# A weight split on one Trainium2 core: the rescaling as a leaky rectifier that also places the sign bit, and one VectorE step less

## The chip, the cores and the metric

The kernel runs on one core of a Trainium2 chip. The metric is the device time of one launch in microseconds (us). The kernel before was run three times: 892.18, 892.35 and 892.69 us, median 892.35 us.

## What is computed

The reference runs three layers one after the other. The first is attention in a sliding window of 64 positions (4 batches, 8 heads, 576 positions, head dimension 64). The second is `softplus(x @ w_in) @ w_out` with 512, 2048 and 512 features for 2304 tokens. The third is a gated layer with three weight matrices:

```python
h = x @ w_in
g = np.maximum(h, 0.0) + np.log1p(np.exp(-np.abs(h)))
x = g @ w_out
gate = 1.0 / (1.0 + np.exp(-(x @ w_gate)))
val = x @ w_val
out = gate * val @ w_out2
```

The weights arrive as 64-bit floats, which the kernel reads as pairs of 32-bit words.

## The kernel before, in words

**Products.** Every product is made with three matrix multiplies, since each factor is split into a high part and a low part (`mm3`, L405 to L408: high by high, high by low, low by high). The first layer runs in five token blocks of 512, 384, 384, 512 and 512 (`BLOCKS1`). For each block and each of 16 slices `f` of the hidden features, `m1_proj(b, f)` makes 12 multiplies into one of two PSUM banks (`h0`, `h1`, chosen by `f % 2`). Then `m1_act` (L435) is the Softplus on ScalarE, `g_hi` (L442) rounds to the high part on ScalarE, `g_lo` (L448) takes the low part on VectorE, and `m1_out(b, f)` makes 12 multiplies into the four accumulators. TensorE runs `m1_proj(f)`, `m1_out(f - 2)`, `m1_proj(f + 1)` and so on in a fixed list (`slots`). Therefore `m1_proj(f + 2)` needs the bank that `g_lo(f)` frees.

**Attention.** The eight groups of block 0 are worked at the start. Those of a later block `b` are worked in the time of block `b - 1`: scores (TensorE, L290), maximum (VectorE, L304 and L307), exponentials (ScalarE, L317, four per group), sum and reciprocal (VectorE, L325 and L326), scaling (GpSimd, L331). Then the probabilities are transposed. For block 1 that is four multiplies on TensorE per group (L339) and a copy (L368); for later blocks VectorE and DMAs do it. The products with the values follow on TensorE (L388), then `att_hi` (L397) and `att_lo` (L402).

**Weights.** Weights come in pairs of 128x512 (two single ones at the start, and single ones for the last matrix). `w_load` (L136) loads them on SyncE's queue. Then five steps make the two parts. `w_scale` (L161, ScalarE) takes the upper word as a 32-bit float and multiplies by 2 to the minus 112, which moves the exponent. `w_shift` (L165, VectorE) shifts the result left by three bits. `w_sign` (L169, VectorE) puts the sign bit of the upper word in. `w_low` (L174, VectorE) puts the three upper bits of the lower word in. `w_hi` (L180, ScalarE) rounds to the high part, and `w_lo` (L188) takes the low part, once per weight. The weights of the first layer are made while block 0 runs. In the time of blocks 1 to 4 the gate and value weights go through the same steps up to `w_low` and then into sums that are sent to DRAM (`c_sums`, `c_hi`, `c_lo`, `c_send`). The twelve single weights of the last matrix follow after that.

**Order.** Each engine runs its instructions in the order in which they are written. Up to the end of the first layer that order comes from a planner, `lead_in` (L957). It asks `traits` (L799) for each step's engine, its estimated time, what it needs and which buffers it takes, derives due times backward from TensorE's list, and then places the step that can start soonest, or the most urgent of those that can start almost as soon. For ScalarE it tells two kinds apart, `"act exp"` and `"act soft"`, and adds 1.3 us (`SWITCH`) where the kind changes; `w_scale` is plain `"act"`:

```python
if engine == "act" and need and need[0] != table:
    us += SWITCH
```

The ACT_TABLE_LOAD instructions themselves are placed when the program is built; the kernel writes one only, at L1030.

Of the kernel before, what the change touches and what calls it, by code (L numbers as in the profile page):

```python
# [9 lines left out]
F32 = mybir.dt.float32  # L10
# [3 lines left out]
AF = mybir.ActivationFunctionType  # L14
ALU = mybir.AluOpType
# [27 lines left out]
def tile_kernel(ctx: ExitStack, tc: tile.TileContext, qk, vt, w1, w2, wg, wv, wo, out):  # L43
# [20 lines left out]
    nc = tc.nc  # L64
# [50 lines left out]
    pair_t, raw_t, bits_t, w_t = {}, {}, {}, {}  # L115

    def pair(slot, turn, dtype, *shape):
        key = slot // 2, turn
        if key not in pair_t:
            pair_t[key] = wpool.tile([P, 2, *shape], dtype, tag=f"w{slot // 2}", name=f"w{slot // 2}", bufs=1)  # L120
        return pair_t[key]

    def size(i):
        return 2 if 1 < i < WO_AT else 1
# [13 lines left out]
    def raw(i, k):  # L138
        r = raw_t[i - i % 2].rearrange("p c (n two) -> p c n two", two=2)
        return r[:, i % 2:i % 2 + size(i), :, k]  # L140

    def bits(i):
        if i == 1:
            bits_t[i] = bits_t["first"][:, 1:]
        if i not in bits_t:
            u, n = i // 2, size(i)
            if u < 3:
                t = main.tile([P, 2, DM], U32, tag="g", name="bits", bufs=GB)
                bits_t.setdefault("first", t)
            elif 4 <= u < 14:  # L150
                slot = 14 + u % 4 // 2 if u < 12 else 15
                t = pair(2 * slot, -20 - u // 2, U32, 2 * DM)[:, u % 2].rearrange("p (c n) -> p c n", c=2)
            else:
                t = main.tile([P, 2, DM], U32, tag="bits", name="bits", bufs=1)
            bits_t[i] = t[:, :n]
        return bits_t[i]
# [1 line left out]


    def w_scale(i):  # L160
        nc.scalar.activation(out=bits(i).bitcast(F32), in_=raw(i, 1).bitcast(F32), func=AF.Copy, scale=2.0 ** -112)  # L161

    def w_shift(i):
        t = bits_t[i]
        nc.vector.tensor_scalar(out=t, in0=t, scalar1=3, scalar2=None, op0=ALU.logical_shift_left)  # L165

    def w_sign(i):
        t = bits_t[i]
        nc.vector.scalar_tensor_tensor(out=t, in0=raw(i, 1), scalar=0x80000000, in1=t, op0=ALU.bitwise_and,  # L169
                                       op1=ALU.bitwise_or)  # L170

    def w_low(i):
        t = bits_t[i]
# [457 lines left out]
    def at(slot, order, fn, *args):  # L631
        events[slot].append((order, len(events[slot]), fn, args))
# [50 lines left out]
    for b in range(1, NB1):  # L683
        s0, s1 = pos[m1_proj, b - 1, 0], pos[m1_proj, b, 0]
        ng, g0 = BLOCKS1[b] // Q, starts1[b] // Q
        for j in range(ng):
            far = b >= FAR
            first = -3 if far else 9
            t = s0 + first + (s1 - s0 - (14 if far else 15 + first)) * (j // 2) // max(ng // 2 - 1, 1)
# [4 lines left out]
    def weight(i, t):  # L694
        for k in range(size(i)):
            at(t - 2, 50, w_load, i + k)
        at(t, -20, w_scale, i)
        at(t + 1, -20, w_shift, i)
        at(t + 1, -19, w_sign, i)
        at(t + 1, -18, w_low, i)  # L700
        at(t + 2, -20, w_hi, i)
        for k in range(size(i)):
            at(t + 2, -19, w_lo, i + k)

    for i in (0, 1, *range(2, len(seq1), 2)):
        weight(i, i + LAG - (i < 3) * (3 - i) - LEAD)
# [3 lines left out]
    def used_last(slot):  # L710
        return max(pos[m1_proj if kind == "w1" else m1_out, NB1 - 1, f]
                   for (kind, f), _ in seq1[slot - slot % 2:slot - slot % 2 + 2])

    for f in range(NF2):
        t, i = COMBO0 + int(COMBO * f), len(seq1) + 2 * f
        at(t - 2, -60, w_load, i)
        at(t - 1, -60, w_load, i + 1)
        at(t, -20, w_scale, i)
        at(t + 1, -20, w_shift, i)
        at(t + 1, -19, w_sign, i)  # L720
        at(t + 1, -18, w_low, i)
        at(t + 3, -15, c_sums, f)
        at(t + 4, -15, c_sum4, f)
        for k, part in enumerate(("a", "v", "x", "s4")):
            at(t + 2 + k, -14, c_hi, f, part)
            at(t + 2 + k, -13, c_lo, f, part)
            at(t + 6 + k, -61, c_send, f, part)
    for f in range(NF2):
        i = WO_AT + f
        t = end + (-7, -1)[f] if f < 2 else pos[m2_out, 0, f - 2, 0] - 1  # L730
        t0 = t - 8
        assert used_last(place[i]) < t < pos[m2_out, 0, f, 0] - 4, (f, used_last(place[i]), t, pos[m2_out, 0, f, 0])
        at(t0, -60, w_load, i)
        at(t, -20, w_scale, i)
        at(t + 1, -20, w_shift, i)
        at(t + 2, -20, w_sign, i)
        at(t + 3, -20, w_low, i)
        at(t + 4, -20, w_hi, i)
        at(t + 4, -19, w_lo, i)
    at(last + 4, -62, wc_load, 0, 0)  # L740
    at(end, -62, wc_load, 0, 1)
    for s in range(NS2):
        t = last + 2 if s == 0 else pos[m2_prod, s - 1, 3, 0]
# [5 lines left out]
    for k in range(7):  # L749
        for kc in range(2):  # L750
            t = max(used_last(2 * k + kc) + 1, last + 18 + k)
# [27 lines left out]
    for g in range(NG0):  # L779
        t = int(first + RG * g)  # L780
# [18 lines left out]
    def traits(fn, a, *rest):  # L799
# [71 lines left out]
            return "act", 0.12 + 0.48 * size(a), deps, ring  # L871
        if fn is w_shift:
            return "dve lock", 0.15 + 0.27 * size(a), [(w_scale, a)], []
        if fn in (w_sign, w_low):
            return "dve lock", 0.15 + 0.54 * size(a), [(w_shift if fn is w_sign else w_sign, a)], []
        if fn is w_hi:
            deps, u = [(w_low, a)], a // 2
            if a >= WO_AT:
# [78 lines left out]
    def lead_in():  # L957
# [5 lines left out]
        for t in sorted(events):  # L963
            if t < end:
                us = when[t] if t >= 0 else OPEN + 2.9 * t
                for order, n, fn, args in sorted(events.pop(t), key=lambda e: e[:2]):
                    nodes[fn, *args] = [us + order / 400, *traits(fn, *args)]
# [122 lines left out]
```

## Time and profile before

| | |
|---|---|
| median of three runs | 892.35 us |
| profiled execution, own time | 892.14 us |
| its span | 890.3 us |
| granted TensorE clock, mean | 0.999 of full speed |
| TensorE busy | 882.0 us, 99% of the span |
| VectorE busy | 522.9 us, 59% |
| ScalarE busy | 398.2 us, 45% |
| GpSimd busy | 154.7 us, 17% |
| DMA | 177.57 MB, mean 199 GB/s |

The profile shows one execution. "Busy" counts time in instructions that compute; a multiply's end is modelled, so 99% for TensorE says that it hardly ever stood still. The span is the time from the first to the last profiled instruction; what the metric has beyond it (1.84 us here) lies around the program. PE is TensorE, DVE is VectorE, ACT is ScalarE, POOL is GpSimd and SP is SyncE.

### The profile page before, as it was taken

The numbers are of one execution on the slowest core, as the hardware profiler recorded it, in microseconds if no ns is written. First come the engines' busy times: TensorE is split into PE (matmuls) and PEld (weight loads), VectorE is DVE, ScalarE is ACT, GpSimd is POOL, SyncE is SP. The second block draws the span as 40 slices with busy tenths as digits, with TensorE's granted clock in tenths as the row PEclk, the third lists the DMA queues.
The fourth block names the chain that finished last, engine by engine and source line by source line (L and its number), as shares of the span: only waits on it lengthen the run. The fifth ranks groups of instructions, "written<-read, shape, count | busy, mean of one in ns | idle before, by whom it ended". The sixth has DMA issues, their size and how long they took to land.

```text
span 890.3 us, 13467 instructions
## 1 busy us (share of the span) xinstructions
PE 882.0 (99%) x5035; PEld 795.9 (89%) x5035; DVE 522.9 (59%) x907; ACT 398.2 (45%) x878; POOL 154.7 (17%) x157
## 2 busy tenths in 40 slices
PE   9999999999999999999999999999999999999997
PEld 7788889999999888888889999999999999999996
DVE  5899976556646657365515667667445447444444
ACT  6867866537755656245323333334222225122222
POOL 4001201102110121003001233331111112111110
PEclk9999999999999999999999999999999999999999
DMA  9946446657886764773306665545454445444441
GB/s 349 396 160 219 136 161 219 244 171 248 270 267 229 234 229 157 229 261 131 131 18 242 243 252 206 201 179 212 185 204 156 156 157 221 173 166 166 166 166 72
DMA packets 56209, 177.57 MB, mean 199 GB/s; under 512 B 6096, under 2 KB 21456, under 8 KB 51536
## 3 DMA queue, kind: packets, MB, share of 16 engines
q1 hardware_dynamic: 56000, 176.58, 56.0%
q8 instruction: 40, 0.66, 0.3%
q14 instruction: 25, 0.20, 0.1%
q10 hardware_dynamic: 144, 0.13, 0.0%
HBM read 139.72 MB, written 36.96 MB: 198 GB/s over the span
## 4 chain that ended last, share of the span: by engine, by line
PE 93%; DMA 4%; DVE 2%; ACT 1%; issue 0%; SPq 0%; ACTq 0%
PE h L406 17%; PE h L408 17%; PE h L407 17%; PE acc L406 11%; PE acc L407 11%; PE acc L408 11%; PE at L290 2%; PE at L408 2%; PE at L407 2%; PE at L406 2%; PE at L388 2%; DMA raw<-in_w 1%; DMA w<-in_w 1%; DMA w<-in_vt 1%; DMA w<-in_qk 1%; DVE w L174 0%
## 5 line engine op out<-in xcount | busy, mean ns | idle before, releaser
L524 DVE TENSOR_TENSOR w<-h,w 128x384 f32<-128x384 f32 x216 | 117.1, 556 | 160.1 <-PE h L408 157.4
L406 PE MATMUL h<-w,wc 128*128 128x384 f32 x504 | 169.0, 335 | 0.1
L408 PE MATMUL h<-w,wc 128*128 128x384 f32 x504 | 169.0, 335 | 0.0
L407 PE MATMUL h<-w,wc 128*128 128x384 f32 x504 | 168.8, 335 | 0.0
L536 POOL TENSOR_TENSOR g<-w,g 128x384 fp32r<-128x384 f32 x70 | 74.0, 1057 | 296.8 <-ACT g L529 252.1
L406 PE MATMUL h<-xt,w 128*128 128x512 f32 (+1 forms) x320 | 119.1, 372 | 0.4 <-ACT w L180 0.3
L406 PE MATMUL acc<-g,w 128*128 128x512 f32 (+1 forms) x320 | 119.4, 373 | 0.0
L408 PE MATMUL h<-xt,w 128*128 128x512 f32 (+1 forms) x320 | 117.9, 368 | 0.5 <-DVE w L188 0.5
L408 PE MATMUL acc<-g,w 128*128 128x512 f32 (+1 forms) x320 | 117.6, 368 | 0.0
L407 PE MATMUL acc<-g,w 128*128 128x512 f32 (+1 forms) x320 | 117.6, 368 | 0.0
L407 PE MATMUL h<-xt,w 128*128 128x512 f32 (+1 forms) x320 | 117.6, 368 | 0.0
L448 DVE TENSOR_TENSOR g<-h,g 128x512 fp32r<-128x512 f32 (+1 forms) x80 | 50.7, 633 | 83.3 <-ACT g L442 82.9
L406 PEld LDWEIGHTS h<-w,wc 128*128 128x128 f32 x504 | 94.6, 188 | 2.3 <-DVE w L524 0.4
L407 PEld LDWEIGHTS h<-w,wc 128*128 128x128 f32 x504 | 94.6, 188 | 2.0
L408 PEld LDWEIGHTS h<-w,wc 128*128 128x128 f32 x504 | 94.6, 188 | 0.0
L529 ACT CAST g<-w 128x384 fp32r<-128x384 f32 x72 | 36.9, 513 | 119.1 <-DVE w L524 119.1
L435 ACT ACTIVATE h<-h 128x512 f32<-128x512 f32 (+1 forms) x80 | 43.2, 540 | 104.6 <-PE h L408 104.3
L408 PEld LDWEIGHTS h<-xt,w 128*128 128x128 f32 x320 | 60.1, 188 | 8.9 <-DVE w L188 1.4
L406 PEld LDWEIGHTS h<-xt,w 128*128 128x128 f32 x320 | 60.1, 188 | 8.6 <-issue 0.6
L331 POOL TENSOR_TENSOR p<-p,st 128x512 f32<-128x512 f32 (+1 forms) x28 | 29.2, 1049 | 220.8 <-DVE st L326 107.6
L406 PEld LDWEIGHTS acc<-g,w 128*128 128x128 f32 x320 | 60.1, 188 | 7.7
L408 PEld LDWEIGHTS acc<-g,w 128*128 128x128 f32 x320 | 60.1, 188 | 7.5
(129 smaller groups left out, 1433.6 us busy)
## 6 DMA issues: line engine op xcount, KB each, us to landing
wc<-wcd SPq DMA_DIRECT2D x36, 1792.0 KB, 7.4
qk<-in_qk SPq DMA_DIRECT2D x28, 512.0 KB, 4.9
wcd<-raw SPq DMA_DIRECT2D x24, 512.0 KB, 3.2
w<-in_w SPq DMA_DIRECT2D x16, 512.0 KB, 9.2
raw<-in_w SPq DMA_DIRECT2D x16, 512.0 KB, 4.6
v<-in_vt SPq DMA_DIRECT2D x25, 256.0 KB, 3.6
raw<-in_wg SPq DMA_DIRECT2D x12, 512.0 KB, 5.1
raw<-in_wv SPq DMA_DIRECT2D x12, 512.0 KB, 6.7
```

What stands on the lines that cost most here:

```text
L290: nc.tensor.matmul(out=s[:, j, :w], lhsT=t[:, 0, j, :], rhs=t[:, 1, j, :w], start=g >= NG0, stop=g >= NG0 or j == NPAIR - 1)
L331: nc.gpsimd.tensor_tensor(out=p[:, :, :w], in0=p[:, :, :w], in1=st[:, 2, :].unsqueeze(2).to_broadcast([P, NPAIR, w]), op=ALU.mult)
L388: nc.tensor.matmul(out=o[h * Q:(h + 1) * Q, j, k * Q:(k + 1) * Q], lhsT=v[:w, (2 * j + h) * Q:(2 * j + h + 1) * Q], rhs=pt[:w, h, j], star ...
L406: nc.tensor.matmul(out=o, lhsT=lh, rhs=rh, start=first, stop=False)
L407: nc.tensor.matmul(out=o, lhsT=lh, rhs=rl, start=False, stop=False)
L408: nc.tensor.matmul(out=o, lhsT=ll, rhs=rh, start=False, stop=last)
L435: nc.scalar.activation(out=t, in_=t, func=AF.Softplus)
L448: nc.vector.tensor_tensor(out=g[:, 1, :n], in0=t, in1=g[:, 0, :n].bitcast(F32), op=ALU.subtract)
L524: nc.vector.tensor_tensor(out=out, in0=a, in1=b, op=op)
L529: nc.scalar.copy(out=g[:, 0, :HALF], in_=t)
L536: eng.tensor_tensor(out=g[:, 1, :HALF], in0=t, in1=g[:, 0, :HALF].bitcast(F32), op=ALU.subtract)
```

## The change

`w_scale` no longer uses Copy but Prelu, a rectifier with a slope of its own for negative inputs. A positive word is multiplied by 2 to the minus 112 as before. A negative one is multiplied further by minus 2 to the 32: the result is positive, and its exponent is larger by 32. The shift by three bits carries that bit of the exponent into the place of the sign. `w_sign` is removed, with its three calls and its place in `traits`; `w_low` now follows `w_shift` directly, also in the planner. Nothing else in the planner's table is edited: `w_scale` stays plain `"act"` with the same estimated time.

```diff
     def w_scale(i):
-        nc.scalar.activation(out=bits(i).bitcast(F32), in_=raw(i, 1).bitcast(F32), func=AF.Copy, scale=2.0 ** -112)
+        nc.scalar.activation(out=bits(i).bitcast(F32), in_=raw(i, 1).bitcast(F32), func=AF.Prelu, scale=2.0 ** -112,
+                             alpha=-2.0 ** 32)
...
-    def w_sign(i):
-        t = bits_t[i]
-        nc.vector.scalar_tensor_tensor(out=t, in0=raw(i, 1), scalar=0x80000000, in1=t, op0=ALU.bitwise_and,
-                                       op1=ALU.bitwise_or)
...
         at(t + 1, -20, w_shift, i)
-        at(t + 1, -19, w_sign, i)
         at(t + 1, -18, w_low, i)
...
         at(t + 1, -20, w_shift, i)
-        at(t + 2, -20, w_sign, i)
         at(t + 3, -20, w_low, i)
...
-        if fn in (w_sign, w_low):
-            return "dve lock", 0.15 + 0.54 * size(a), [(w_shift if fn is w_sign else w_sign, a)], []
+        if fn is w_low:
+            return "dve lock", 0.15 + 0.54 * size(a), [(w_shift, a)], []
```

## Rows read from the trace of the kernel before

**Rows 1.** The page: busy time of the engines (share of the span), instructions.
```profile
PE 882.0 (99%) x5035; PEld 795.9 (89%) x5035; DVE 522.9 (59%) x907; ACT 398.2 (45%) x878; POOL 154.7 (17%) x157
```

**Rows 2.** Timeline of TensorE: start, length, line, tile; idle before and releaser in brackets.
```profile
27.18 2.76 PE L418 MATMUL h<-idle 128*128 128x512 bf16 x12
30.10 0.47 PE L406 MATMUL h<-xt,w 128*128 128x512 f32 x1
...
37.79 0.50 PE L406 MATMUL h<-xt,w 128*128 128x512 f32 x1 [0.26 <-ACT w L180]
...
93.38 0.50 PE L408 MATMUL h<-xt,w 128*128 128x512 f32 x1 [0.53 <-DVE w L188]
```

**Rows 3.** Stages: stretch, its length, busy of PE, PEld, DVE, ACT, POOL (counts).
```profile
34.00:66.00 32.00, 31.74 (x147) 26.14 (x147) 29.85 (x41) 23.60 (x43) 0.00 (x0) 1.00 0.63 226
66.00:106.00 40.00, 39.47 (x251) 32.75 (x250) 36.50 (x57) 32.91 (x66) 7.16 (x6) 1.00 0.54 181
130.00:370.00 240.00, 240.00 (x1579) 223.52 (x1578) 137.53 (x253) 141.29 (x338) 35.49 (x34) 1.00 0.68 226
475.00:890.00 415.00, 410.45 (x2149) 382.55 (x2148) 227.08 (x408) 119.11 (x238) 88.84 (x82) 1.00 0.50 185
```

**Rows 4.** Stages, VectorE's sign step (L169) alone: stretch, its length, busy (count).
```profile
0.00:106.00 106.00, 16.37 (x14) 1.00 0.71 255
106.00:890.00 784.00, 27.31 (x27) 1.00 0.55 192
```

**Rows 5.** SyncE's queue: what the weight loads waited for (us, times, longest).
```profile
SPq L136 <- DVE w L174: 41.4, 8, 12.6
```

**Rows 6.** ScalarE's groups by line: the table loads (busy, mean ns, idle before).
```profile
L435 ACT ACT_TABLE_LOAD x15 | 19.2, 1283 | 0.3
L317 ACT ACT_TABLE_LOAD x14 | 18.0, 1283 | 0.8 <-DVE st L307 0.5
```

**Rows 7.** Timeline of ScalarE, 65 to 85 us, columns as in Rows 2.
```profile
65.38 0.58 ACT L435 ACTIVATE h<-h 128x512 f32<-128x512 f32 x1
65.99 0.59 ACT L442 CAST g<-h 128x512 fp32r<-128x512 f32 x1
66.48 1.14 ACT L161 ACTIVATE w<-raw 128x1024 f32<-128x1024 f32 x1
...
68.45 0.59 ACT L435 ACTIVATE h<-h 128x512 f32<-128x512 f32 x1
...
69.56 1.15 ACT L161 ACTIVATE w<-raw 128x1024 f32<-128x1024 f32 x1
73.78 0.58 ACT L435 ACTIVATE h<-h 128x512 f32<-128x512 f32 x1 [3.08 <-PE h L408]
...
75.82 1.18 ACT L161 ACTIVATE w<-w 128x1024 f32<-128x1024 f32 x1
...
80.11 0.58 ACT L435 ACTIVATE h<-h 128x512 f32<-128x512 f32 x1 [1.05 <-PE h L408]
...
82.79 1.28 ACT L317 ACT_TABLE_LOAD   x1 [0.53 <-DVE st L307]
84.09 0.40 ACT L317 ACTIVATE p<-p,st 128x128 f32<-128x128 f32 x1
```

**Rows 8.** Timelines of GpSimd and TensorE: the scaled probabilities and their transposes.
```profile
88.03 3.02 POOL L331 TENSOR_TENSOR p<-p,st 128x512 f32<-128x512 f32 x2 [18.20 <-DVE st L325]
...
91.35 1.03 PE L339 MATMUL at<-ident,p 128*128 128x128 f32 x8
```

**Rows 9.** Timelines of ScalarE, VectorE, TensorE: a combined weight's scaling at 266 us.
```profile
267.55 0.48 ACT L435 ACTIVATE h<-h 128x384 f32<-128x384 f32 x1
...
268.65 1.18 DVE L169 SCALAR_TENSOR_TENSOR bits<-raw,bits 128x1024 uint32<-128x1024 uint32 x1
...
271.01 0.55 DVE L448 TENSOR_TENSOR g<-h,g 128x384 fp32r<-128x384 f32 x1
...
272.31 0.33 PE L406 MATMUL h<-xt,w 128*128 128x384 f32 x1
```

More of the change, by code (lines that the diff above doesn't have):

```diff
@@ L719, in tile_kernel @@
         at(t + 1, -20, w_shift, i)
-        at(t + 1, -19, w_sign, i)
         at(t + 1, -18, w_low, i)
```

## Prediction

> **What bounds the kernel now.** I read the page first. TensorE is busy 882.0 us, 99% of the span [rows 1], so a change pays only where TensorE stands still, and costs only where it makes TensorE stand still. I then asked the timeline of TensorE for its idle stretches between the first product of the first layer (30.10 us) and the last product. Two are worth naming: 0.26 us at 37.79, ended by a weight's high part on ScalarE, and 0.53 us at 93.38, ended by a weight's low part on VectorE [rows 2]. The rest is in tenths; the 4.55 us that it lacks after 475 us [rows 3] lie almost wholly behind the last product, at the output. So a faster weight path can give back about 0.8 us; with the two pairs of multiplies around these waits, whose starts are spread by some 0.3 us more, about 1.1 us.
>
> The table by stages says which engine is near its limit. From 34 to 106 us, while the first layer's weights are made, VectorE is busy 29.85 of 32 and 36.50 of 40 us, ScalarE 23.60 and 32.91 [rows 3]. VectorE is the tighter one, but ScalarE's idle time is only 8.40 + 7.09 = 15.5 us. From 130 to 370 us both have room: VectorE 57% and ScalarE 59% busy.
>
> **What goes: the sign step.** It stands 41 times, 16.37 us before 106 us and 27.31 us after, 43.7 us in all [rows 4]. After 106 us it lies beside a TensorE that does not wait for it, so it is worth nothing there. Before 106 us it lies on the busiest helper, and the weights come some 1.2 us per pair earlier from VectorE (1.18 is the length of one in [rows 9]). That is worth at most the 1.1 us above. It has a second effect: eight weight loads wait on SyncE's queue until the step w_low has freed the raw buffer, 41.4 us together [rows 5]. They start earlier, and the DMA engines have room for them, 0.54 of their time in use from 66 to 106 us [rows 3]. So w_scale becomes possible earlier, which spreads the work of ScalarE a little better.
>
> **What is added: Prelu in place of Copy, at the same 41 places.** The instruction itself I cost at nothing: a Softplus on 128x512 takes 0.58 us and a cast of the same size 0.59 [rows 7], so the function does not set the length. The question is the table. Here the trace shows three things. Copy (L161) stands between Softpluses without a load [rows 7]. Exp and Softplus never share a table: 14 loads lead to Exp and 15 back to Softplus [rows 6]. And a change of table takes 1.30 us, from 82.79 to 84.09, with nothing further between the neighbours [rows 7]. Prelu is in no row. Its bounds are: no load at all (like Copy), or a load before and one after it, 2.60 us, wherever it stands between two Softpluses (like Exp). I take the second. Copy and cast only scale and convert; Prelu chooses a slope by the sign of each element, so its nearest relative in the trace is a function with a curve, and all such functions here that differ have paid.
>
> The Trainium skill ("ScalarE: Activation LUTs", Table sets: the hidden batching unit) says that cheap functions such as relu, copy, identity and abs are in every set, and that calls should be batched by set. Read so that Prelu counts with relu, no load would come; that is the rival "no loads" below. The same page (What ACT_TABLE_LOAD costs) puts a switch at about 2.66 us, a 1283 ns load and a drain of about 1380 ns; this trace has the 1283 ns but 1.30 us in all, so by the page a pair would be 5.3 us and by the row 2.60. The row decides.
>
> **How many loads, and where.** In the order of before, w_scale stands between two Softpluses at 6 places from 34 to 106 us (66.48, 69.56 and 75.82 are three of them [rows 7]), and at 13 later ones up to 450 us; at four others it stands beside Exp or is followed by it and costs nothing more. The planner knows nothing of Prelu's table, so it won't gather them. That is 19 x 2.60 = 49 us of ScalarE. In the first stage it is 6 x 2.60 = 15.6 us against 15.5 us of idle time: no reserve is left.
>
> **What TensorE feels in the first stage.** I walk ScalarE's row [rows 7] with 1.30 us per change. The Softplus at 68.45 starts 2.6 us late. The next one had waited 3.08 us for TensorE, so of 5.2 us it is 2.1 late. The one at 80.11 had 1.05 us of waiting: 2.1 + 2.6 - 1.05 = 3.65 us late. No Softplus itself stops TensorE at that, because a bank is wanted again only after three more sets of 12 multiplies. But the exponentials follow: with the 0.53 us before their load taken off they are 3.1 us late. Their scaling on GpSimd ended at 88.03 + 3.02 = 91.05; 3.1 us later is 94.15. TensorE wanted the second group's transposes half a microsecond into the row at 91.35, at about 91.85 [rows 8], and everything behind them stands in its queue. It waits 2.3 us. The wait of 0.53 us at 93.38 is then covered: net 1.8 us. The next group of exponentials (100 us) is in the same position with one place more before it; I add 0.2 us. The upper end is all 15.6 us, the lower end is none, if the earlier weights let w_scale move into the idle 8.4 us before 66 us. I take 2.0: with no reserve on ScalarE the walk is the nearer end.
>
> **Later.** At 266 us the Softplus would be 2.6 us late, and TensorE wanted that bank at 272.31, 0.75 us after the low part of 271.01 ended. But that low part stood behind the sign step and w_low on VectorE; without the 1.18 us of the sign step it still comes in time [rows 9]. At the other 12 places the same three timelines show the bank free 2.8 to 8 us before TensorE wants it. A newly dealt order may be less lucky once: I take 0.4 us, between 0 and 13 x 2.6 = 34. After 475 us ten w_scale stand among Sigmoids; ScalarE is busy 119.11 of 415 us there [rows 3], and even with two loads each (26 us) it has room: nothing. The 0.26 us at 37.79 I leave, because the Softplus before it sets the same moment. Sum: 2.0 + 0.4 = +2.4 us.
>
> **The rivals.** A measurement of this kernel tells about 0.2%, 1.8 us, from no change.
>
> 1. *Covered.* The loads come, but the earlier weights and the idle time take them up. For it: VectorE is freed by 16.37 us before 106, SyncE's loads move ahead [rows 4, 5]. Against it: the exponentials hang on TensorE's scores, not on weights, and are in ScalarE's queue behind every Prelu. It decides if they start less than 0.8 us late. Time: -1.1 to +1.7, say 892.4 us.
> 2. *ScalarE becomes the bound of the first stage.* Earlier weights bring more w_scale between the Softpluses than before, up to one for each pair. Eight or nine places instead of 6 are 21 to 23 us against 15.5 of idle time, so 5 to 8 us spill over onto TensorE: 897 to 901, say 899.0 us.
> 3. *No loads.* Prelu sits in Softplus's table. Then only the gain is left, 0.8 to 1.1 us of 1.1: 891.5 us. For it is the skill's sentence on cheap functions, against it that each function with a curve here has paid.
> 4. *Faster by more than 1.8 us.* The 1.1 us cannot do it alone; the first product at 30.1 us would have to start a microsecond earlier as well, since two sign steps stand before it on VectorE. Against it: twelve multiplies of constants (L418), 2.76 us, end 0.16 us before it [rows 2]. 890.3 us.
>
> **How the numbers follow.** Forecast as summed: 0.44, by itself 893.9 to 897. Covered 0.30, ScalarE bound 0.12, no loads 0.08, faster 0.06. Slower is 0.44 + 0.12 = 0.56, same 0.30 + 0.08 = 0.38, faster 0.06. The sum is made on the profiled execution: 892.14 + 2.4 = 894.5; the median of the runs is 0.2 us above that execution, so 894.7 us. The range goes from 891.2, where most of "no loads" and all but the best of "covered" is in, to 900.0, in the upper half of "ScalarE bound"; the 0.06 of "faster" and some 0.08 at the edges are left out.
>
> **What would show it.** Right: some 40 more ACT_TABLE_LOADs, now with L161 as their line too; about 50 us more ScalarE; VectorE 44 us less; an idle stretch of TensorE near 91 or 107 us ended by GpSimd's scaling or by ScalarE; no change after 475 us. Wrong: as many loads as before (then rival 3), or 40 more and no such idle stretch (rival 1), or idle stretches at many Softpluses from 38 us on (rival 2).

## The result, and the profile after

The changed kernel takes 900.84 us, the median of four runs (899.69 to 901.3), against 892.42 us for the kernel before in the same series. The ratio is 1.0092 with a 95% interval of 1.0075 to 1.011: slower by 8.4 us. The forecast was 894.7 us with a range up to 900.0, so the direction was right and the size was too small by more than a factor of three. The profiled execution took 901.3 us with a span of 899.1 us, 8.8 us more than the span of before.

First the page of the changed kernel, its busy times and the granted clock in 40 slices.

```profile
PE 884.9 (98%) x5035; PEld 796.2 (89%) x5035; DVE 477.7 (53%) x864; ACT 445.5 (50%) x914; POOL 157.7 (18%) x161
...
PEclk9998999999999999999999999999999999999999
```

Against [rows 1] VectorE is busy 45.2 us less and ScalarE 47.3 us more. The clock has a dent in the fourth slice, which covers 67 to 90 us. The groups by line of ScalarE say where its 47 us come from (busy, mean ns of one, idle before):

```profile
L431 ACT ACT_TABLE_LOAD x34 | 43.6, 1283 | 0.6
L161 ACT ACT_TABLE_LOAD x22 | 28.2, 1283 | 15.8 <-DMA raw<-in_wv 13.6 <-issue 1.0 <-DVE w L184 0.9
L161 ACT ACTIVATE bits<-raw 128x1024 f32<-128x1024 f32 (+1 forms) x26 | 23.8, 914 | 0.2
L313 ACT ACT_TABLE_LOAD x11 | 14.1, 1283 | 0.5 <-DVE st L303 0.4
```

There are 69 table loads instead of 31 (two single ones are not among these lines): 38 more, and 22 of the 69 stand before Prelu (L161), which had none as Copy [rows 6, 7]. None of the 22 lies after 475 us, where ten rescalings stand among Sigmoids. The instruction itself costs what Copy cost: the 26 of the group shown take 914 ns on average, and as Copy took 912 ns. The next rows are the table by stages (stretch, length, busy of PE, PEld, DVE, ACT, POOL, then the granted clock):

```profile
34.00:66.00 32.00, 32.00 (x151) 26.77 (x150) 23.63 (x37) 29.34 (x47) 1.61 (x2) 1.00 0.74 265
66.00:106.00 40.00, 35.22 (x188) 28.85 (x187) 28.09 (x42) 36.08 (x53) 2.08 (x2) 0.91 0.47 165
130.00:370.00 240.00, 238.56 (x1576) 221.63 (x1576) 128.80 (x245) 162.66 (x365) 41.60 (x39) 1.00 0.71 230
475.00:899.00 424.00, 419.56 (x2191) 390.15 (x2189) 219.52 (x403) 120.80 (x241) 88.90 (x83) 1.00 0.51 185
```

Compare with [rows 3]. ScalarE and VectorE have changed places: from 34 to 66 us VectorE falls from 29.85 to 23.63 and ScalarE rises from 23.60 to 29.34. TensorE loses its time from 66 to 106 us, where it stands still for 4.8 us of 40 and runs at a mean clock of 0.91. After 475 us it lacks 4.4 us, as before. TensorE's timeline shows the place (start, length, idle before and its releaser):

```profile
78.31 0.50 PE L402 MATMUL h<-xt,w 128*128 128x512 f32 x1 [1.38 <-DVE g L444]
...
84.73 3.78 PE L286 MATMUL at<-qk 128*128 128x128 f32 x16 [3.40 <-ACT pt L364]
88.17 0.77 PE L402 MATMUL acc<-g,w 128*128 128x512 f32 x1
...
90.31 0.40 PE L404 MATMUL acc<-g,w 128*128 128x512 f32 x1
```

It waits 1.38 us for the bank that a late Softplus had not given back, and then 3.40 us for the copy of the transposed probabilities. Behind the second wait it is slow. The next two lines are 16 score multiplies of the kernel before, and the table by stages of the changed kernel from 85 to 90 us, where the granted clock is 0.50:

```profile
79.91 1.95 PE L290 MATMUL at<-qk 128*128 128x128 f32 x16
...
85.00:90.00 5.00, 5.00 (x20) 4.63 (x21) 2.44 (x5) 3.98 (x5) 0.00 (x0) 0.50 0.35 112
```

The 16 score multiplies take 3.78 us, where those of the kernel before took 1.95 us, and five of the long multiplies take 2.14 us from 88.17 to 90.31, where five at 0.23 us are 1.15 us. So the slow stretch costs 1.8 + 1.0 = 2.8 us more. ScalarE's timeline just before shows why everything came late:

```profile
67.05 1.28 ACT L431 ACT_TABLE_LOAD   x1
68.34 0.58 ACT L431 ACTIVATE h<-h 128x512 f32<-128x512 f32 x1
68.95 0.59 ACT L438 CAST g<-h 128x512 fp32r<-128x512 f32 x1
69.56 1.28 ACT L161 ACT_TABLE_LOAD   x1
70.85 1.14 ACT L161 ACTIVATE w<-raw 128x1024 f32<-128x1024 f32 x1
71.88 1.15 ACT L161 ACTIVATE w<-w 128x1024 f32<-128x1024 f32 x1
72.91 1.06 ACT L176 CAST w<-w 128x1024 fp32r<-128x1024 f32 x1
73.85 1.17 ACT L161 ACTIVATE w<-w 128x1024 f32<-128x1024 f32 x1
75.04 1.28 ACT L431 ACT_TABLE_LOAD   x1
76.34 0.58 ACT L431 ACTIVATE h<-h 128x512 f32<-128x512 f32 x1
...
83.15 1.04 ACT L176 CAST w<-w 128x1024 fp32r<-128x1024 f32 x1 [0.87 <-DVE w L170]
84.10 1.05 ACT L364 COPY pt<-at 128x512 f32<-128x512 f32 x2
```

ScalarE does not rest from 53.7 us to the Softplus at 76.34. That Softplus belongs to a product whose last multiply ended at 67.6 us. In between, the planner had dealt three rescalings and a cast in one row, as if they cost nothing but themselves. The low part, the weights' casts and VectorE's w_low are then late in turn, and the copy that TensorE needs at 81.3 us stands behind the last of those casts.

The waits and the slow stretch add up: 1.4 + 3.4 + 2.8 = 7.6 us in the first stage, and two waits of 0.9 and 0.4 us later, 8.9 us. The two waits of [rows 2], 0.8 us, are gone. That leaves 8.1 of the 8.8 us of span; the rest is spread in tenths.

### The profile page after: what moved, and what is told of

Read it like the earlier page. It is cut to its first block, busy times and chain, and to the rows that moved or that the text cites. A ratio compares the mean times of both kernels' runs of the same rounds, so it can differ in the third digit from the quotient of the medians.

```text
span 899.1 us, 13486 instructions
## 1 busy us (share of the span) xinstructions
PE 884.9 (98%) x5035; PEld 796.2 (89%) x5035; DVE 477.7 (53%) x864; ACT 445.5 (50%) x914; POOL 157.7 (18%) x161
## 4 chain that ended last, share of the span: by engine, by line
PE 82%; ACT 8%; DMA 4%; DVE 3%; issue 2%; SPq 1%; POOL 0%; ACTq 0%; POOLq 0%
PE h L402 15%; PE h L404 15%; PE h L403 15%; PE acc L402 9%; PE acc L404 9%; PE acc L403 9%; PE at L286 2%; PE at L404 2%; PE at L403 2%; PE at L402 2%; PE at L384 2%; ACT p L313 2%; DMA raw<-in_wv 2%; DMA pd<-pd 1%; ACT L431 1%
## 5 line engine op out<-in xcount | busy, mean ns | idle before, releaser
L558 ACT ACTIVATE w<-w 128x384 f32<-128x384 f32 x36 | 19.0, 527 | 105.9 <-DVE w L520 105.8
L402 PEld LDWEIGHTS h<-xt,w 128*128 128x128 f32 x320 | 60.1, 188 | 10.4 <-DVE g L444 2.5
L402 PEld LDWEIGHTS acc<-g,w 128*128 128x128 f32 x320 | 60.4, 189 | 8.5 <-ACT x L462 0.8
L404 PEld LDWEIGHTS acc<-g,w 128*128 128x128 f32 x320 | 60.3, 188 | 7.7
L403 PEld LDWEIGHTS acc<-g,w 128*128 128x128 f32 x320 | 60.4, 189 | 7.3
```

What stands on the lines that cost most here:

```text
L402: nc.tensor.matmul(out=o, lhsT=lh, rhs=rh, start=first, stop=False)
L403: nc.tensor.matmul(out=o, lhsT=lh, rhs=rl, start=False, stop=False)
L404: nc.tensor.matmul(out=o, lhsT=ll, rhs=rh, start=False, stop=last)
L558: nc.scalar.activation(out=sb, in_=u2, func=AF.Sigmoid)
```

## The experiments

The theory after this reading was *loads*: the 38 table loads make ScalarE late, and nothing else matters. The rival was *order*: the planner deals the steps differently without the sign step, and that order is worse by itself.

**1. The changed order without the loads.**

```diff
-        nc.scalar.activation(..., func=AF.Prelu, scale=2.0 ** -112, alpha=-2.0 ** 32)
+        nc.scalar.activation(..., func=AF.Copy, scale=2.0 ** -112)
```

> The changed kernel with Copy in place of Prelu: the order of all instructions stays, only the table loads go. The sign step is still gone, so the negative weights lose their sign. Theory 'loads': the 38 extra table loads are the whole loss, and the time falls to 891.3 to 892.6 us, with 31 loads and no TensorE wait above 0.6 us after 38 us. Rival 'order': the planner's newly dealt order is worse by itself, and the time stays at 898 us or more with the 3.4 us wait near 81 us still there.

Measured: 891.04 us, ratio 0.9984 (0.9975 to 0.9994), with 31 loads again. Its page and TensorE's waits (line, releaser, us in total, times, longest):

```profile
PE 880.9 (99%) x5035; PEld 794.7 (89%) x5035; DVE 476.9 (54%) x864; ACT 396.7 (45%) x876; POOL 159.3 (18%) x161
...
PE h L413 <- DVE idle L411: 2.0, 1, 2.0
PE acc L285 <- DMA w<-in_qk: 0.4, 1, 0.4
PE acc L334 <- POOL w L326: 0.3, 1, 0.3
```

All three waits lie before the first layer's first product. So the order is not worse: it is 1.4 us better, and the loads on top of it cost 900.84 - 891.04 = 9.8 us. *Order* falls.

**2. The order of before with the loads.** The kernel before, with Prelu for Copy and the sign step kept.

> The kernel before with Prelu in place of Copy and the sign step kept: the order of before, plus the loads. Theory 'loads': some 38 more loads on the old order; by the walk of the prediction 2 to 3 us late, 894.7 us; up to 900 us if the order does not matter and loads alone set the loss. Rival 'order': 892.4 us, as before.

Measured: 903.7 us, ratio 1.0133 (1.0116 to 1.015). This is the order whose first stage the prediction had walked through by hand, with the sign step still in place. It is 11.3 us slower, not 2.4, and above both expectations. Its TensorE waits show what the walk had missed:

```profile
PE h L409 <- DVE w L189: 6.1, 6, 2.6
...
PE acc L407 <- ACT x L467: 1.0, 1, 1.0
```

Six waits are for a weight's low part on VectorE (L189). None of the six is for the transposes. VectorE's timeline before the longest, at 76.94 us, and before the one at 125.70 us shows a chain:

```profile
75.59 0.69 DVE L449 TENSOR_TENSOR g<-h,g 128x512 fp32r<-128x512 f32 x1 [4.16 <-ACT g L443]
76.20 0.68 DVE L189 TENSOR_TENSOR w<-w,w 128x512 fp32r<-128x512 f32 x1
...
124.35 0.69 DVE L449 TENSOR_TENSOR g<-h,g 128x512 fp32r<-128x512 f32 x1 [1.98 <-ACT g L443]
124.96 0.68 DVE L189 TENSOR_TENSOR w<-w,w 128x512 fp32r<-128x512 f32 x1
```

VectorE runs its list in order. It stood 4.16 us for the g_lo of a late Softplus, and the w_lo behind that, whose own input had been there since 73.05 us, stood with it. These two waits (2.6 and 0.9 us) are 3.5 of the 6.1 us. Before the other four VectorE was busy with earlier steps of its list up to the low part itself. Behind the longest wait the clock fell as well: nine multiplies from 77.74 to 81.39 us take 1.6 us more than nine at 0.23 us. The first two experiments, with the two kernels, make a table: Copy with the sign step 892.4, Copy without 891.04, Prelu with it 903.7, Prelu without it 900.84. Taking the sign step away is worth 1.4 us without loads and 2.9 us with them.

**3. The planner told.**

```diff
-            return "act", 0.12 + 0.48 * size(a), deps, ring
+            return "act exp", 0.12 + 0.48 * size(a), deps, ring
```

> The changed kernel with one word in the planner's table: w_scale is of the kind 'act exp', so the planner sees the change of table and its 1.3 us. Theory 'loads': the planner gathers the rescalings next to each other and next to the exponentials, 45 to 60 loads instead of 69, and the time falls to 892 to 896 us. Rival 'order': another deal with no reason to be better, 897 us or more.

Measured: 894.22 us (893.32 to 896.48), ratio 1.0024 (1.0015 to 1.0034). The time is in the range expected, and the reason given for it is wrong, as the loads by line and the stage from 34 to 106 us show:

```profile
L431 ACT ACT_TABLE_LOAD x35 | 44.9, 1283 | 0.6
L161 ACT ACT_TABLE_LOAD x21 | 26.9, 1283 | 13.8 <-DMA raw<-in_wv 13.6
L313 ACT ACT_TABLE_LOAD x13 | 16.7, 1283 | 0.2
```

```profile
34.00:106.00 72.00, 72.00 (x403) 60.42 (x402) 54.03 (x81) 69.31 (x105) 3.74 (x4) 1.00 0.57 199
```

There are 71 loads, two more than in the changed kernel. ScalarE is busy 69.31 of 72 us, and TensorE does not stand still at all. The planner gathered nothing. It spread the rescalings, nearly everywhere one between two Softpluses where the changed kernel has up to three, and in this stage TensorE waits for nothing that stands behind them. So the number of loads does not set the loss; loads that the order does not reckon with do, as the pair of this kernel and the changed one shows. The profiled run took 893.51 us. What it loses after 130 us begins with one wait of 1.2 us at 283 us, of which more in experiment 7, and one of 0.5.

**4. The copies on VectorE.**

```diff
-COPIES = ("act", 0.55), ("dve", 0.69)
+COPIES = (("dve", 0.69),)
```

> The changed kernel with the copies of the transposed probabilities (L364) fixed to VectorE; the planner deals anew. If the 3.4 us wait near 81 us comes from the copy's place behind ScalarE's late weight casts alone, it goes, with the slow clock behind it, and the time falls to 894 to 896 us. If ScalarE as a whole is late, the wait moves to the exponentials or to a Softplus, and the time stays at 898 us or more.

Measured: 897.24 us, ratio 1.0055 (1.0041 to 1.0068), between the two expectations. The wait stayed in its place with another name, while the 1.4 us wait before it went:

```profile
PE at L286 <- DVE pt L364: 3.6, 1, 3.6
```

ScalarE has the same three rescalings in one gap (69.07 to 73.2 us). VectorE stood 2.26 us for the g_lo behind it, and the copies, at 82.38 us, came after eight more of its steps. So the place of the copy was not the cause; what is late is everything behind that gap, on either engine.

**5 and 6. The change for a part of the weights.** One kernel makes it for the first layer's weights alone, the other for the combined weights and the last matrix alone; the others keep Copy and the sign step.

```diff
+    def prelu(i):
+        return i < len(seq1)    # experiment 5; 6: i >= len(seq1)
...
-            at(t + 1, -19, w_sign, i)
+            if not prelu(i):
+                at(t + 1, -19, w_sign, i)
```

> The change made for the first layer's weights only (i < 32); the 12 combined pairs and the last matrix keep Copy and the sign step. Theory 'first stage': the loss is made where ScalarE has no reserve, before 130 us, so most of the 8.4 us stays: 897.5 to 900 us. Rival 'every pair of loads costs the same': 12 of some 19 load places are gone, so about a third of the loss stays: 894.5 to 896 us.

> The reverse: Copy and sign step for the first layer's weights, the change for the 12 combined pairs and the last matrix. Theory 'first stage': 892.4 to 894.5 us, with at most two TensorE waits of about 1 us after 130 us. Rival 'every pair costs the same': 897 to 898.5 us.

Measured: 898.61 us for the first layer (ratio 1.0064, 1.0052 to 1.0077), and 899.37 us for the later ones (1.0073, 1.006 to 1.0086). The first is as the theory had it: with 43 loads (31 before) it has the same two waits, 1.4 and 3.4 us, as the changed kernel, which is 2.2 us slower still. The second lies outside both expectations. I had expected at most two waits of about 1 us. The later weights have only 51 loads and lose 6.9 us by themselves, nearly as much as all together. The parts do not add up, because each kernel gets an order of its own.

The second kernel's runs lay between 896.73 and 900.38 us, and its profile was of the fastest, so it was profiled once more.

> The later-weights-only kernel once more, for its profile: its five runs lay between 896.7 and 900.4 us and the profiled one was the fastest. If the waits seen there (1.4 us at 176, 2.7 us at 399) are the whole loss in every run, this one is at 896 to 897.5 us. If a slower run has more or longer waits, or a lower TensorE clock behind one of them, it is at 898 to 901 us and its profile shows which.

Measured: 899.23 us. TensorE's timeline around 400 us, first of the 896.73 us run, then of the 899.23 us run:

```profile
401.91 0.50 PE L410 MATMUL acc<-g,w 128*128 128x512 f32 x1 [2.54 <-DVE x L472]
...
404.09 0.39 PE L410 MATMUL acc<-g,w 128*128 128x512 f32 x1
```

```profile
402.91 0.50 PE L410 MATMUL acc<-g,w 128*128 128x512 f32 x1 [2.60 <-DVE x L472]
...
404.43 0.63 PE L412 MATMUL acc<-g,w 128*128 128x512 f32 x1
404.85 0.63 PE L410 MATMUL acc<-g,w 128*128 128x512 f32 x1
```

The wait is the same. In the first run the multiplies go on at one in 0.23 us, in the second at one in 0.43 us until 407.3 us; the mean clock from 400 to 410 us is 1.00 in the one and 0.83 in the other. The eight slow multiplies from 404.00 to 407.35 cost 3.35 - 8 x 0.23 = 1.5 us more. The spans differ by 2.5 us; 0.8 us of that is already there at the first product (30.86 against 30.02 us). What TensorE waits for is a copy of an accumulator, at the end of a block, behind this piece of ScalarE's list:

```profile
392.45 1.28 ACT L165 ACT_TABLE_LOAD   x1 [1.36 <-DMA raw<-in_wv]
393.74 1.12 ACT L165 ACTIVATE bits<-raw 128x1024 f32<-128x1024 f32 x1
...
398.04 1.28 ACT L439 ACT_TABLE_LOAD   x1
399.33 0.58 ACT L439 ACTIVATE h<-h 128x512 f32<-128x512 f32 x1
```

VectorE's copy (401.17 us) stood behind the g_lo of that Softplus (400.56 us), the same pattern as in experiment 2.

**7. The first layer alone, with the planner told.**

> As the first-layer-only kernel, and the planner knows that these rescalings need the table of Exp. The run with the planner told everywhere had no TensorE wait before 130 us and lost 1.4 us at 282 and 0.6 at 399. If those two come from the combined pairs' loads, they go here and only the gain of the sign step is left: 891.0 to 892.2 us. If telling the planner costs something of its own, or the waits come from the new deal, 893 to 895 us.

Measured: 894.24 us (892.99 to 896.35), ratio 1.0018 (1.0009 to 1.0027): the second case. The wait at 282 us is still there, although no combined weight causes a load here. ScalarE's timeline:

```profile
282.54 0.39 ACT L321 ACTIVATE p<-p,st 128x128 f32<-128x128 f32 x1
282.93 0.56 ACT L401 CAST xt<-at 128x512 fp32r<-128x512 f32 x1
283.39 0.40 ACT L321 ACTIVATE p<-p,st 128x128 f32<-128x128 f32 x1
```

The cast that ends the attention of the next block (L401) stands among exponentials, and TensorE waits 1.2 us for it. That is an accident of the new deal; no Prelu and no load of one stands near it. So the part of the told kernels' loss that lies here is one of order, not of tables. The profile is of the fastest of eleven runs, which spread over 3.4 us. The five up to 893.64 us show a mean granted clock of 0.999 or 1.000, the six from 894.24 us on 0.996 to 0.998. So part of the spread is time at the lower clock, as in experiment 6; behind which wait it fell no profile shows.

**8. Where Prelu costs no load.** The change for the first five rescalings alone, which all run before the first Softplus (`i < 8`, planner told).

> Prelu and no sign step for the first five rescalings alone (i = 0, 1, 2, 4, 6), which run before the first Softplus and so under Exp's table: no load more than before. All other weights as before. If the gain of the sign step (1.3 us with no loads at all) is made at the start, where a weight's high part is waited for at 37.8 us, 891.5 to 892.1 us; if it needs the later pairs too, 892.2 to 892.6 us.

Measured: 891.49 us (891.17 to 891.78 in eleven runs), ratio 0.9988 (0.9978 to 0.9997), at the edge of the first expectation. It is faster than both kernels, by 1.0 us against the kernel before. Its loads by line and TensorE's waits:

```profile
L439 ACT ACT_TABLE_LOAD x16 | 20.5, 1283 | 0.3
L321 ACT ACT_TABLE_LOAD x15 | 19.2, 1283 | 1.5 <-DVE st L311 1.3
...
PE h L412 <- DVE w L192: 0.3, 1, 0.3
```

None of the 33 loads stands before a Prelu (two more than before lead to Exp and back), the wait of 0.26 us of [rows 2] is gone and that of 0.53 is 0.3. Most of what the sign step is worth without loads (1.4 us) is got from five of the 41 places.

**9. A dearer switch in the planner.** Experiment 3 with `SWITCH` at 2.6 instead of 1.3 us.

> The kernel with the planner told, and the planner's price for a change of table doubled from 1.3 to 2.6 us. If fewer changes are what counts, the planner gathers more rescalings (60 loads or fewer instead of 71) and the time falls below 894.2 us, to 892 to 893.5. If it is enough that the planner expects the delay, the count stays near 71 and the time within 2 us of 894.2.

Measured: 907.51 us, ratio 1.0173 (1.0146 to 1.0199), slower than every other kernel here, and outside both expectations. The loads do become fewer, 65. TensorE's two largest waits:

```profile
PE h L402 <- DVE g L444: 6.8, 5, 2.2
PE h L404 <- DVE w L184: 2.7, 2, 2.2
```

Five waits are for a g_lo. From 130 to 370 us alone TensorE stands still for 7.7 of 240 us, where experiment 3 has 1.4. So an order that reckons with the loads can still be a bad one; this deal, at twice the price, is the worst of all. Which of the planner's choices does it was not tried.

## Why the prediction was right or wrong

**What bounds the kernel: right.** The time was lost where TensorE stood still or ran slowly, from 66 to 106 us above all.

**The sign step's worth: right, a little low.** At most 1.1 us was forecast; experiment 1 shows 1.4. VectorE's busy time fell by 45.2 us (44 forecast). From 130 to 370 us TensorE is busy all 240 us in experiment 1 as in the kernel before [rows 3], so the step's absence is worth nothing there.

**Prelu needs its own table between Softpluses: right.** Rival 3, *no loads*, is excluded: 38 more loads, where some 40 were forecast, and ScalarE 47.3 us busier, where it was about 50. Beside Exp it costs no load (in the changed kernel a Prelu at 92.38 us is followed by Exp at 93.46), and beside Sigmoid none either. The sentence of the Trainium skill ("ScalarE: Activation LUTs", Table sets: the hidden batching unit) that cheap functions are in every set does not extend to Prelu and Softplus here; its rule that calls should be batched by set fits experiment 8, and experiment 3 shows that it is not the only way.

**1.30 us for a change of table: right.** The changed kernel goes from the cast at 68.95 (to 69.54) over the load at 69.56 to the Prelu at 70.85. The 2.66 us of the Trainium skill ("ScalarE: Activation LUTs", What ACT_TABLE_LOAD costs) did not appear.

**What TensorE feels in the first stage, 2.0 us: this step failed.** The changed kernel lost 7.6 us there, 6.8 without the 0.8 us of the two waits that went; experiment 2, in the order that the step had walked through, cost 11.3 us in all. The step had three faults. It followed one chain, exponentials to transposes, to its end, and took the sentence "No Softplus itself stops TensorE at that" as enough for the others. But the 1.38 us wait of the changed kernel is for just such a Softplus's bank, and VectorE's list is run in order as well: in experiment 2 a late Softplus holds up g_lo, and a weight's low part stands behind that g_lo although its own input is there (two waits, 3.5 us). The idle stretch near 91 us that GpSimd's scaling was to end did not appear in either kernel. The step used the places of before, while the new order put three rescalings into one gap. And it knew no price for the clock: in the changed kernel 2.8 us of the 7.6 come after the wait and not in it.

**Later, 0.4 us: this term was too small.** TensorE of the changed kernel stands still for 1.4 us from 130 to 370 us, where it did not stand still before, and the kernel is 2.2 us slower than experiment 5. In another order the later weights alone cost 6.9 us (experiment 6). I had looked at the bank that each Softplus must free, and not at the copies of the accumulators at the end of a block (2.5 us in experiment 6) or at the ends of the attention (0.9 us in the changed kernel).

**The rivals.** The time lies in the range of rival 2, *ScalarE becomes the bound of the first stage*, to which I gave 0.12 and 899.0 us, but its mechanism did not show. It asked for eight or nine places between Softpluses; the changed kernel loads a table for Prelu at seven places from 34 to 106 us, and six of these lie between two Softpluses, as many as the forecast had counted. It asked for idle stretches at many Softpluses; there are two, both behind one gap. Nor does a busy ScalarE decide: experiment 3 loads a table for Prelu at eight places there, with ScalarE at 96% of its time and TensorE at 100%. What made the difference is that the order did not reckon with the loads, which the prediction had stated ("The planner knows nothing of Prelu's table") and then not used for the size. Two pairs of kernels differ only in what the planner is told of the loads: the changed kernel and experiment 3 (900.84 and 894.22 us), experiments 5 and 7 (898.61 and 894.24 us). Experiment 9 shows that it is not enough, and what else makes an order good stays open.

## What to carry to other kernels

Before a function on ScalarE is exchanged, look at which functions stand around it in its list: a function with another table can cost two loads at each place, and where the order is planned by estimates, the estimate has to say so, with the time that was measured. To size a delay, follow every engine that runs its list in order behind the delayed one, and price the slow multiplies behind a wait of some microseconds too. A change that loses everywhere may still win in the few places where its price is not charged, as the first five rescalings here.

## What the runs showed of the hardware

After a wait of 2.5 to 3.4 us TensorE's granted clock fell in some cases and not in others. In the changed kernel it stood at half, the 1.2 GHz level, from 85 to 90 us (0.50 in the table by stages), behind 3.40 us of idle time, and the wait of 1.38 us six microseconds before left it at full speed. In experiment 6 the same wait of 2.5 to 2.6 us was followed by full speed (1.00 from 400 to 410 us) in one run and by slow multiplies (0.83) in the next.

A change of table on ScalarE takes 1.30 us from one instruction to the next, and what it costs the kernel depends on what stands behind it: 71 loads in experiment 3 left TensorE without a pause from 34 to 106 us. Prelu had to load beside Softplus (22 times in the changed kernel) and not beside Exp or Sigmoid, and Copy, at the same 41 places, never.
